# A delta-rule recurrence followed by a token mixer on one core: loads, decay factors, key transposes and mixer products placed differently

## The chip, the cores and the metric

One core of a Trainium2 chip runs the whole program. The metric is device time in microseconds (us). PE is the matmul engine, PEld its weight load, DVE the vector engine, ACT the engine for activation functions, POOL the GpSimd engine; SP only issues DMAs. Each engine works through its own instructions in the order in which they are queued.

## The reference

For 4 batches, 8 heads, 768 tokens and head size 40 (all float32):

```python
for t in range(S):
    y[:, :, t] = einsum('bhd,bhde->bhe', r_t, state)
    Sa = einsum('bhde,bhe->bhd', state, a_t)
    state = state * w_t[:, :, None, :] - einsum('bhd,bhe->bhde', Sa, b_t) + einsum('bhd,bhe->bhde', v_t, k_t)
x = y.transpose(0, 2, 1, 3).reshape(B, S, 320)
theta = x @ w_theta
zr, zi = x * cos(theta), x * sin(theta)
u = x + einsum('ts,bsd->btd', w_tok_r, zr) + einsum('ts,bsd->btd', w_tok_i, zi)
out = u + maximum(u @ w_ch, 0)
```

## The kernel before

The tokens are cut into 24 tiles of 128 (6 to a batch, in order), and one loop, `for i in range(N)`, takes a tile per step with all 8 heads. Inside a tile the recurrence is a masked product of matrices; from tile to tile goes the state `gt`.

- **Load** (`load`, L128): six DMAs of 160 KB for a tile, issued by SP in the order w, k, b, a, r, v. Pool `raw` has three buffers of each, so a tile's buffers come free when the tile three before it has been read. Step i asks for tile i+4.
- **Prepare**: `prep_ln` (ACT, L134) takes the logarithm of w; `prep_csi` sums it with a matmul (L148), takes the Exp (ACT, L151) and multiplies k and b by it (POOL, L155: `kb`); `prep_cse` does the like with the sum that excludes the token itself (L162 to L168, Exp L174) and multiplies a (POOL, L176: `ah`). `prep_rv` (POOL, L143) casts r and v to bf16. `tr_kb`, `tr_rv`, `tr_a` transpose them on PE (L182); the copies out of PSUM are on DVE (L193: `kbT`) and ACT.
- **Scores**: `sc_psiphi` and `sc_lams` (PE, L214) each make two 128x1024 products, and DVE masks them (L222: psi, phi, lamv, lamu). They go in turn through two PSUM tiles named `sc`; everything else in PSUM goes in turn through four named `sm`.
- **Recurrence**: `rec_x0` (L263, L269) gives `nx` (ACT, L273), `rec_nu` gives `nu`, `rec_gt` the next state, `rec_gd` its transpose. `out_y` and `out_xt` make the tile's x and its transpose, one step late.
- **Mixer**: `moe_theta` (PE L410, copy L424) runs for tile i-2 in step i. Twice per batch (at its tile 4, and at tile 1 of the next) `moe_sines` takes cosine and sine of three tiles' theta (ACT, L443), which needs another activation table; `ln_exp_again` (L447) loads the first one again. `moe_z` (POOL, L432: `zr`, `zi`) multiplies them with x one step later, six products in a row. From step 9 on a step has one row block of the mixer, from step 21 on two: `moe_y` (12 matmuls, L453), `moe_ut` (L362) and, a step later, `moe_ch` (L410) and the output DMA.
- **Weights**: after step 0 POOL issues the DMAs of w_theta and w_ch; after each of steps 0 to 5 those of one row block of both token weights (`wtok_load`, L375, two of 128x768). `wtok_trans` (PE L399, DVE L402) transposes a block two steps after its load.
- **Tail**: after the loop the last batch's theta, sines, products and six row blocks are left.

The order in which an engine's instructions are queued is not quite the order of the program: a planner at compile time follows the program but lets a later instruction go first when, by its own estimate of times, the earlier one is not ready. `keep_in_program_order` holds the marked instructions in the program's order. So a cast or product may be queued ahead of one that the program has before it, and then the engine waits for it.

Of the kernel before, what the change touches and what calls it, by code (L numbers as in the profile page):

```python
# [18 lines left out]
def kernel(  # L19
# [63 lines left out]
    for i, t in sorted(to_zero, key=lambda e: e[0]):  # L83
        nc.vector.memset(t, 0.0)

    raw = ctx.enter_context(tc.tile_pool(name="raw", bufs=3))
    exps = ctx.enter_context(tc.tile_pool(name="exps", bufs=4))
    trs = ctx.enter_context(tc.tile_pool(name="trs", bufs=3))
    scs = ctx.enter_context(tc.tile_pool(name="scs", bufs=2))
# [18 lines left out]
    def tile_of(pool, shape, dt, tag):  # L108
        return pool.tile(shape, dt, name=tag, tag=tag)
# [26 lines left out]
    def prep_rv(i):  # L136
        q = tiles[i]
        q.rvb = rv_t[i % NB]
        for j in range(2):
            if i < 2:  # L140
                nc.scalar.copy(out=q.rvb[:, j, :, 0:D], in_=q.rv[:, j])
            else:
                nc.gpsimd.tensor_copy(out=q.rvb[:, j, :, 0:D], in_=q.rv[:, j])  # L143

    def prep_csi(i):
        q = tiles[i]
        csi = tile_of(ps_sm, [128, 512], FP32, "sm")
        nc.tensor.matmul(csi[:, 0:DM], lhsT=ntri_inc, rhs=q.lw[:, :, 0:D],  # L148
                         start=True, stop=True)
        q.invW = tile_of(exps, [128, 1, H, D], FP32, "invW")  # L150
        nc.scalar.activation(out=q.invW.rearrange("p o h d -> p (o h d)"),  # L151
                             in_=csi[:, 0:DM], func=AF.Exp)
        q.kbh = kb_t[i % NB]
        for j in range(2):
            (nc.vector if i < 2 else nc.gpsimd).tensor_tensor(  # L155
                out=q.kbh[:, j, :, 0:D], in0=q.kb[:, j], in1=q.invW[:, 0],
                op=ALU.mult)

    def prep_cse(i):
# [13 lines left out]
        q.Wi = tile_of(exps, [128, DM + 8], FP32, "Wi")
        nc.scalar.activation(out=q.Wi, in_=cse[:, 0:DM + 8], func=AF.Exp)  # L174
        q.ah = ah_t[i % 2]
        (nc.vector if i < 2 else nc.gpsimd).tensor_tensor(  # L176
            out=q.ah[:, :, 0:D], in0=q.a,
            in1=q.Wi[:, 0:DM].rearrange("p (h d) -> p h d", h=H), op=ALU.mult)
# [238 lines left out]
    def moe_theta(i):  # L417

        bi, j = divmod(i, NCH)
        if bi not in ths:  # L420
            ths[bi] = tile_of(mk, [128, NT, DM], FP32, "th")
        tp = tile_of(ps_sm, [128, 512], FP32, "sm")
        mix3(tp[:, 0:DM], tiles[i].xT, wth)
        nc.scalar.copy(out=ths[bi][:, j], in_=tp[:, 0:DM])  # L424

    cs_of = {}

    def moe_z(bi, js):
        cs = cs_of[bi, js[0]]
        for m, j in enumerate(js):  # L430
            for c in range(2):
                nc.gpsimd.tensor_tensor(out=zs[bi][c][:, j], in0=cs[:, c, m],  # L432
                                        in1=tiles[bi * NCH + j].x, op=ALU.mult)

    def moe_sines(bi, js):
        if bi not in zs:
            zs[bi] = (tile_of(mk, [128, NT, DM], BF16, "zr"),
                      tile_of(mk, [128, NT, DM], BF16, "zi"))
        j0, n = js[0], len(js)
        cs = tile_of(mk, [128, 2, 3, DM], FP32, "cs")  # L440
        cs_of[bi, j0] = cs
        for c in range(2):
            tc.keep_in_program_order(nc.scalar.activation(  # L443
                out=cs[:, c, 0:n], in_=ths[bi][:, j0:j0 + n], func=AF.Sin,
                bias=(pi2_col[:, :], 0.0)[c]))
# [61 lines left out]
    prep_cse(1)  # L507
    lv = score(tiles[0].rvT[:, 1], tiles[0].rvT[:, 0])
    tiles[0].lamv = masked("lamv", lv, mask_p)
    tr_kb(1)  # L510
    prep_rv(1)
    tr_rv(1)
    prep_ln(2)
    prev = []
    z_due = None
    for i in range(N):
        bi, ci = divmod(i, NCH)
        yrows = rows_at.get(i, [])
        sines = ci == 4 or (ci == 1 and bi > 0)
        nxt(load, i + 4)  # L520
        rec_x0(i)
        nxt(tr_a, i + 1)
        if i > 1:
            moe_theta(i - 2)
        nxt(prep_csi, i + 2)
        rec_nu(i)
        if i > 0:
            out_y(i - 1)
        nxt(prep_cse, i + 2)
        nxt(sc_psiphi, i + 1)  # L530
        out_nut(i)
        rec_gt(i)
        nxt(ev_phi, i + 1)
        if i > 0:
            out_xt(i - 1)
        due = None
        if sines:
            due = (bi, (0, 1, 2)) if ci == 4 else (bi - 1, (3, 4, 5))
            moe_sines(*due)
            ln_exp_again()  # L540
            busy_act[0] = True
        for m in prev:
            moe_ch(*m)
        nxt(prep_rv, i + 2)
        for m in yrows:
            moe_y(*m)
        nxt(tr_rv, i + 2)
        nxt(tr_kb, i + 2)
        sc_lams(i, i + 1)
        rec_gd(i)  # L550
        for m in yrows:
            moe_ut(*m)
        busy_act[0] = False
        if i == 0:
            moe_weights()
        if i < NCH:
            wtok_load(i)
        if 2 <= i < NCH + 2:
            wtok_trans(i - 2)
        nxt(prep_ln, i + 3)  # L560
        if z_due:
            moe_z(*z_due)
        z_due = due
        prev = yrows
    moe_theta(N - 2)
    moe_sines(B - 1, (3, 4))
    moe_z(B - 1, (3, 4))
    out_y(N - 1)
    for m in prev:
        moe_ch(*m)  # L570
    acc = [tile_of(ps_sc, [128, 2, 512], FP32, "sc") for _ in range(2)]
    yps = [acc[j // 2][:, j % 2, 0:DM] for j in range(4)]
    for j in range(2):
        y_part(yps[j], B - 1, j, range(NT - 1), True, False)
    out_xt(N - 1)
    for j in range(2, 4):
        y_part(yps[j], B - 1, j, range(NT - 1), True, False)
    moe_theta(N - 1)
    moe_sines(B - 1, (5,))
    moe_z(B - 1, (5,))  # L580
    for j in range(NT):
        if j < 4:
            y_part(yps[j], B - 1, j, (NT - 1,), False, True)
            y_evac(yps[j], B - 1, j)
        else:
            moe_y(B - 1, j)
        if j > 0:
            moe_ut(B - 1, j - 1)
        if j > 1:
            moe_ch(B - 1, j - 2)  # L590
    moe_ut(B - 1, NT - 1)
    moe_ch(B - 1, NT - 2)
    moe_ch(B - 1, NT - 1)


# [28 lines left out]
```

## Time and profile before

| | |
|---|---|
| time, median of 3 runs | 260.32 us (259.92 to 261.09) |
| profiled execution: time, span | 262.26 us, 260.5 us |
| busy, of the span | PE 215.0 (83%), DVE 185.4 (71%), ACT 160.4 (62%), POOL 120.9 (46%) |
| loads by SP (queue q1) | 27.54 MB, 59.1% of 16 DMA engines over the span |
| chain that ended last | PE 46%, ACT 15%, issue 12%, DMA 10%, POOL 9% |

The span is what the profiler saw from the first to the last instruction. A step is told here from the end of one `nx` (L273) to the end of the next; step i begins at the end of its own `nx`, and there are 24 of them. A buffer number in a tile's name counts through a ring: `rv_94` to `rv_97` and `kb_90` to `kb_93` are tiles 0 to 3, then 4 to 7, and so on.

### The profile page before, as it was taken

What the parts mean: (1) busy time and instruction counts of PE and PEld (TensorE: products, weight loads), DVE (VectorE), ACT (ScalarE), POOL (GpSimd) and SP (SyncE); (2) the same over time, 40 slices, a digit from 0 to 9 for tenths busy, and PEclk for the clock granted to TensorE, in tenths of its full rate; (3) what the DMA queues carried; (4) which work ended last, traced back from release to release, by engine and by line L of the source; (5) the groups of instructions that cost most, each with busy time, mean ns of one, the idle gap of its engine ahead of it and who ended that gap; (6) DMA issues with size and microseconds to landing.
All of it is one profiled execution on the core that took longest, in us unless ns stands there. A gap on an engine that the chain in (4) does not pass through costs nothing.

```text
span 260.5 us, 8110 instructions
## 1 busy us (share of the span) xinstructions
PE 215.0 (83%) x3368; PEld 167.8 (64%) x3368; DVE 185.4 (71%) x287; ACT 160.4 (62%) x303; POOL 120.9 (46%) x186
## 2 busy tenths in 40 slices
PE   1579968977099969997999899989989999897593
PEld 0457747756067758786777687767777877674361
DVE  5377865887158968897889788978897877750233
ACT  2466645688226867796769576967695838542221
POOL 2009736365735595278427832784177301504200
PEclk9999997999659979999999999999999999999778
DMA  7999999999999898767697579645500001011012
GB/s 128 189 176 149 210 158 195 159 159 169 181 190 168 138 172 154 133 117 136 129 172 138 91 137 169 113 95 110 103 29 4 28 25 35 20 64 40 0 50 101
DMA packets 155685, 30.81 MB, mean 118 GB/s; under 512 B 150401, under 2 KB 155649, under 8 KB 155649
## 3 DMA queue, kind: packets, MB, share of 16 engines
q1 hardware_dynamic: 153216, 27.54, 59.1%
q0 software_dynamic: 2432, 2.77, 6.4%
q8 instruction: 26, 0.43, 0.7%
q14 instruction: 11, 0.08, 0.1%
HBM read 29.13 MB, written 3.93 MB: 127 GB/s over the span
## 4 chain that ended last, share of the span: by engine, by line
PE 46%; ACT 15%; issue 12%; DMA 10%; POOL 9%; DVE 4%; SPq 3%; POOLq 0%; DVEq 0%; ACTq 0%
PE sm L453 10%; DMA raw_rv<-in_r_dram 9%; PE sm L182 7%; PE sc L214 6%; PE sm L410 5%; ACT cs L443 4%; SPq L128 3%; ACT L443 2%; ACT L447 2%; PE sc L453 2%; PE sm L362 2%; PE sm L349 2%; PE sm L278 2%; DVE lamu L222 1%; POOL kb_93 L155 1%
## 5 line engine op out<-in xcount | busy, mean ns | idle before, releaser
L103 ACT COPY rvT<-sm 128x1024 bf16<-128x1024 bf16 x18 | 18.2, 1013 | 26.0 <-PE sm L182 26.0
L453 PE MATMUL sm<-zr,wtok_r 128*128 128x320 bf16 x120 | 33.8, 304 | 0.0
L453 PE MATMUL sm<-zi,wtok_i 128*128 128x320 bf16 x120 | 33.7, 303 | 0.0
L222 DVE TENSOR_TENSOR psi<-sc,mask_p 128x1024 bf16<-128x1024 f32 x24 | 29.3, 1221 | 5.4 <-PE sc L214 5.1
L222 DVE TENSOR_TENSOR phi<-sc,mask_n 128x1024 bf16<-128x1024 f32 x24 | 29.1, 1214 | 0.0
L222 DVE TENSOR_TENSOR lamu<-sc,mask_p 128x1024 bf16<-128x1024 f32 x24 | 29.1, 1214 | 0.0
L222 DVE TENSOR_TENSOR lamv<-sc,mask_p 128x1024 bf16<-128x1024 f32 x24 | 29.1, 1214 | 0.0
L193 DVE COPY kbT<-sm 128x1024 bf16<-128x1024 bf16 x24 | 16.5, 687 | 14.7 <-PE sm L182 14.7
L331 ACT COPY nuT<-sm 128x512 bf16<-128x512 bf16 x24 | 14.0, 585 | 10.9 <-PE sm L182 10.8
L453 PEld LDWEIGHTS <-wtok_r 128*128 128x128 bf16 x144 | 14.4, 100 | 9.6 <-issue 3.9
L453 PEld LDWEIGHTS <-wtok_i 128*128 128x128 bf16 x144 | 14.3, 100 | 7.5 <-issue 1.9
L214 PE MATMUL sc<-aT,kbT 64*128 64x128 bf16 x384 | 18.8, 229 | 0.0
L273 ACT ACTIVATE nx<-sm 128x320 bf16<-128x320 f32 x24 | 10.4, 432 | 11.5 <-PE sm L269 11.5
L103 ACT COPY uT<-sm 128x384 bf16<-128x384 bf16 x18 | 8.5, 483 | 14.1 <-PE sm L362 14.1
L143 POOL CAST rv_96<-raw_rv 128x320 bf16<-128x320 f32 x12 | 5.4, 453 | 24.5 <-DMA raw_rv<-in_r_dram 21.8
L155 POOL TENSOR_TENSOR kb_93<-raw_kb,invW 128x320 bf16<-128x320 f32 x12 | 10.1, 866 | 13.2 <-ACT invW L151 13.2
L424 ACT COPY th<-sm 128x320 f32<-128x320 f32 x24 | 10.6, 441 | 8.6 <-PE sm L410 8.6
L200 ACT COPY aT<-sm 128x512 bf16<-128x512 bf16 x24 | 14.1, 587 | 2.0 <-PE sm L182 2.0
L155 POOL TENSOR_TENSOR kb_91<-raw_kb,invW 128x320 bf16<-128x320 f32 x10 | 8.4, 861 | 14.4 <-ACT invW L151 14.4
L410 PE MATMUL sm<-wch,uT 128*128 128x320 bf16 x72 | 14.3, 313 | 0.2 <-ACT uT L103 0.2
L174 ACT ACTIVATE Wi<-sm 128x328 f32<-128x328 f32 x24 | 10.7, 448 | 5.9 <-PE sm L168 3.1
L214 PEld LDWEIGHTS <-kbT 64*128 64x128 bf16 x384 | 11.9, 99 | 3.7 <-issue 2.9
(332 smaller groups left out, 689.5 us busy)
## 6 DMA issues: line engine op xcount, KB each, us to landing
raw_w<-in_w_dram SPq DMA_DIRECT2D x24, 160.0 KB, 3.8
raw_kb<-in_k_dram SPq DMA_DIRECT2D x24, 160.0 KB, 3.5
raw_kb<-in_b_dram SPq DMA_DIRECT2D x24, 160.0 KB, 3.6
raw_a<-in_a_dram SPq DMA_DIRECT2D x24, 160.0 KB, 3.9
raw_rv<-in_r_dram SPq DMA_DIRECT2D x24, 160.0 KB, 3.8
raw_rv<-in_v_dram SPq DMA_DIRECT2D x24, 160.0 KB, 3.9
out_dram<-oo SPq DMA_DIRECT2D x24, 160.0 KB, 1.8
wtok_row_r<-in_moe_w_tok_r_dram POOLq DMA_DIRECT2D x6, 192.0 KB, 5.1
```

Of the source, the lines that this page charges most:

```text
L103: nc.scalar.copy(out=out, in_=in_)
L155: (nc.vector if i < 2 else nc.gpsimd).tensor_tensor(out=q.kbh[:, j, :, 0:D], in0=q.kb[:, j], in1=q.invW[:, 0], op=ALU.mult)
L174: nc.scalar.activation(out=q.Wi, in_=cse[:, 0:DM + 8], func=AF.Exp)
L182: nc.tensor.transpose(out=dst[:, g * 128:(g + 1) * 128], in_=src[:, 2 * g:2 * g + 2, :].rearrange("p a b -> p (a b)"), identity=ident)
L193: nc.vector.tensor_copy(out=q.kbT.rearrange("p a b -> p (a b)"), in_=pt)
L200: nc.scalar.copy(out=q.aT, in_=pt[:, 0:512])
L214: nc.tensor.matmul(P[:, p, g, :], lhsT=lhs[rows(p), g * 128:(g + 1) * 128], rhs=rhs[rows(p), g * 128:(g + 1) * 128], start=True, stop=True)
L222: nc.vector.tensor_tensor(out=s.rearrange("p a b c -> p (a b) c"), in0=P.rearrange("p a b c -> p (a b) c"), in1=mask.to_broadcast([128, 2 ...
L331: nc.scalar.copy(out=q.nuT, in_=pt[:, 0:512])
L410: nc.tensor.matmul(dst, lhsT=lhs[:, kt, :], rhs=rhs[:, kt, :], start=kt == 0, stop=kt == 2)
L443: tc.keep_in_program_order(nc.scalar.activation(out=cs[:, c, 0:n], in_=ths[bi][:, j0:j0 + n], func=AF.Sin, bias=(pi2_col[:, :], 0.0)[c]))
L453: nc.tensor.matmul(yp, lhsT=wtok[nm][:, sb, j * 128:(j + 1) * 128], rhs=z[:, sb], start=start and n == 0, stop=stop and n == 2 * len(sbs) - 1)
```

## The change

Loads get a fourth buffer, and the row blocks of the token weights are loaded and transposed later (steps 3 to 8 and 6 to 11 instead of 0 to 5 and 2 to 7). `tr_kb` runs for tile i+1 near the head of step i, where it ran for tile i+2 near its end. `prep_csi` stands behind `out_y`, and it reloads the table when sines ran before it. `prep_ln` stands ahead of the sines. `moe_theta` runs for tile i-1 late in the step. The products of three tiles are put behind three steps (two where the batch's rows come next). `th` and `cs` have one buffer. The tail takes the row blocks in another order, and DVE does some of its products.

```diff
-    raw = ctx.enter_context(tc.tile_pool(name="raw", bufs=3))
+    raw = ctx.enter_context(tc.tile_pool(name="raw", bufs=4))
+    mk1 = ctx.enter_context(tc.tile_pool(name="mk1", bufs=1))      # for th and cs
...
     def prep_csi(i):
...
+        if reload[0]:
+            ln_exp_again()
+            reload[0] = False
         q.invW = tile_of(exps, [128, 1, H, D], FP32, "invW")
-        nc.scalar.activation(...)
+        tc.keep_in_program_order(nc.scalar.activation(...))       # Wi in prep_cse too
...
-    def moe_z(bi, js):
-        for m, j in enumerate(js):
-            for c in range(2):
-                nc.gpsimd.tensor_tensor(out=zs[bi][c][:, j], ...)
+    def moe_z(group, m, other=None):
+        for c in range(2):
+            eng = other if other is not None and c == 0 else nc.gpsimd
+            tc.keep_in_program_order(eng.tensor_tensor(out=zs[bi][c][:, js[m]], ...))
...
-    tr_kb(1)                                   # ahead of the loop
     for i in range(N):
...
         nxt(tr_a, i + 1)
-        if i > 1:
-            moe_theta(i - 2)
-        nxt(prep_csi, i + 2)
+        nxt(tr_kb, i + 1)
         rec_nu(i)
         if i > 0:
             out_y(i - 1)
+        nxt(prep_csi, i + 2)
         nxt(prep_cse, i + 2)
...
             out_xt(i - 1)
+        nxt(prep_ln, i + 3)
         if sines:
             moe_sines(*due)
-            ln_exp_again()
+            z_due += [(due, m) for m in range(3)]
+            reload[0] = True
...
         nxt(tr_rv, i + 2)
-        nxt(tr_kb, i + 2)
+        if i > 0:
+            moe_theta(i - 1)
         sc_lams(i, i + 1)
...
-        if i < NCH:
-            wtok_load(i)
-        if 2 <= i < NCH + 2:
-            wtok_trans(i - 2)
-        nxt(prep_ln, i + 3)
-        if z_due:
-            moe_z(*z_due)
+        if 3 <= i < NCH + 3:
+            wtok_load(i - 3)
+        if 6 <= i < NCH + 6:
+            wtok_trans(i - 6)
+        for e in z_due[:1 if ci not in (2, 3) and i < N - 1 else 3]:
+            moe_z(*e)
+            z_due.remove(e)
-    moe_theta(N - 2)
     moe_sines(B - 1, (3, 4))
-    moe_z(B - 1, (3, 4))
+    moe_z((B - 1, (3, 4)), 0)
+    moe_z((B - 1, (3, 4)), 1, nc.vector)
     out_y(N - 1)
...
     for j in range(2):
-        y_part(yps[j], B - 1, j, range(NT - 1), True, False)
+        y_part(yps[j], B - 1, j, range(3), True, False)
     out_xt(N - 1)
+    for j in range(2):
+        y_part(yps[j], B - 1, j, range(3, NT - 1), False, False)
+    moe_theta(N - 1)
+    moe_sines(B - 1, (5,))
+    moe_z((B - 1, (5,)), 0, nc.vector)
     for j in range(2, 4):
         y_part(yps[j], B - 1, j, range(NT - 1), True, False)
-    moe_theta(N - 1)
-    moe_sines(B - 1, (5,))
-    moe_z(B - 1, (5,))
-    for j in range(NT):
-        if j < 4: ...
-        else:
-            moe_y(B - 1, j)
+    for j in range(4, NT):
+        yps.append(tile_of(ps_sm, [128, 512], FP32, "sm")[:, 0:DM])
+        y_part(yps[j], B - 1, j, range(NT - 1), True, False)
+    for j in range(NT + 2):
+        if j < NT: ...                         # the last of six parts, for all rows
```

## Rows read from the trace of the kernel before

**Rows 1.** The page's 40 slices: granted TensorE clock, DMA busy share, in tenths

```profile
PEclk9999997999659979999999999999999999999778
DMA  7999999999999898767697579645500001011012
```

**Rows 2.** Windows between ends of `nx`: length, busy per engine (count), clock, DMA share, GB/s

```profile
19.14:101.16 82.02, 64.73 (x1127) 51.98 (x1126) 60.16 (x77) 51.95 (x100) 50.59 (x79) 0.90 1.02 169
25.74:32.64 6.90, 6.24 (x119) 4.99 (x119) 6.03 (x8) 4.72 (x11) 5.28 (x9) 1.00 1.27 209
...
32.64:44.15 11.51, 8.48 (x133) 6.92 (x132) 7.77 (x11) 5.12 (x12) 5.80 (x10) 0.85 1.00 171
44.15:51.74 7.59, 6.93 (x135) 5.68 (x135) 5.83 (x8) 5.39 (x13) 3.07 (x5) 1.00 0.94 167
...
61.39:76.19 14.80, 8.08 (x122) 6.26 (x121) 6.90 (x9) 4.72 (x11) 10.71 (x17) 0.68 1.09 182
...
126.70:135.18 8.48, 8.28 (x141) 6.54 (x140) 7.28 (x10) 5.38 (x13) 3.35 (x5) 1.00 0.72 138
135.18:143.99 8.81, 7.40 (x134) 6.08 (x133) 8.06 (x11) 8.32 (x14) 6.28 (x9) 1.00 0.75 140
...
223.80:260.50 36.70, 27.12 (x226) 17.61 (x225) 12.21 (x25) 10.42 (x21) 6.00 (x8) 0.87 0.13 46
```

**Rows 3.** DMA queue of the weights: packets, MB, share of 16 engines

```profile
q0 software_dynamic: 2432, 2.77, 6.4%
```

**Rows 4.** Timeline of POOL: start, duration, engine, line, tiles, [idle before, releaser]

```profile
18.81 0.45 POOL L143 CAST rv_96<-raw_rv 128x320 bf16<-128x320 f32 x1 [16.37 <-DMA raw_rv<-in_r_dram]
...
63.63 0.82 POOL L432 TENSOR_TENSOR zr<-cs,x_102 128x320 bf16<-128x320 f32 x1
...
69.47 0.45 POOL L143 CAST rv_94<-raw_rv 128x320 bf16<-128x320 f32 x1 [1.31 <-DMA raw_rv<-in_r_dram]
...
70.52 1.67 POOL L155 TENSOR_TENSOR kb_93<-raw_kb,invW 128x320 bf16<-128x320 f32 x2
...
74.68 0.45 POOL L143 CAST rv_95<-raw_rv 128x320 bf16<-128x320 f32 x1 [1.67 <-DMA raw_rv<-in_r_dram]
```

**Rows 5.** Timeline of PE in step 5

```profile
71.43 0.61 PE L182 MATMUL sm<-ident,kb_93 128*128 128x128 bf16 x4 [6.33 <-POOL kb_93 L155]
```

**Rows 6.** Timeline of ACT at the end of step 13, one with sines

```profile
141.90 1.28 ACT L447 ACT_TABLE_LOAD   x1
143.19 0.47 ACT L134 ACTIVATE lw_86<-raw_w 128x320 bf16<-128x320 f32 x1
143.57 0.42 ACT L273 ACTIVATE nx<-sm 128x320 bf16<-128x320 f32 x1
```

**Rows 7.** Timeline of PE at the same place

```profile
144.04 0.57 PE L410 MATMUL sm<-wth,xT_3059 128*128 128x320 bf16 x3 [1.43 <-ACT nx L273]
```

**Rows 8.** Groups by line, weight transposes and `kbT`: busy us, mean ns | idle before

```profile
L399 PE MATMUL sm<-ident,wtok_row_r 128*128 128x128 bf16 x36 | 4.0, 249 | 0.0
L402 DVE COPY wtok_r<-sm 128x768 bf16<-128x768 bf16 x6 | 3.3, 546 | 0.0
L193 DVE COPY kbT<-sm 128x1024 bf16<-128x1024 bf16 x24 | 16.5, 687 | 14.7 <-PE sm L182 14.7
```

**Rows 9.** Timeline at the head of step 12, DVE and PE

```profile
126.44 1.21 DVE L222 TENSOR_TENSOR lamu<-sc,mask_p 128x1024 bf16<-128x1024 f32 x1
128.47 0.49 DVE L353 TENSOR_TENSOR x_113<-sm,Wi 128x320 bf16<-128x320 f32 x1 [0.82 <-PE sm L349]
128.53 0.51 PE L214 MATMUL sc<-aT,kbT 64*128 64x128 bf16 x12
```

**Rows 10.** Chain that ended last, in the tail: start, duration, engine, tile, line

```profile
232.87 1.28 ACT L443
...
242.02 0.43 ACT th L424
...
252.61 1.63 PE sm L453 x12
```

More of the change, by code (lines that the diff above doesn't have):

```diff
@@ L143, in prep_rv @@
                 nc.gpsimd.tensor_copy(out=q.rvb[:, j, :, 0:D], in_=q.rv[:, j])
+    reload = [False]
     def prep_csi(i):
@@ L149, in prep_csi @@
                          start=True, stop=True)
+        if reload[0]:
+            ln_exp_again()
+            reload[0] = False
         q.invW = tile_of(exps, [128, 1, H, D], FP32, "invW")
-        nc.scalar.activation(out=q.invW.rearrange("p o h d -> p (o h d)"),
-                             in_=csi[:, 0:DM], func=AF.Exp)
+        tc.keep_in_program_order(nc.scalar.activation(
+            out=q.invW.rearrange("p o h d -> p (o h d)"), in_=csi[:, 0:DM],
+            func=AF.Exp))
         q.kbh = kb_t[i % NB]
@@ L173, in prep_cse @@
         q.Wi = tile_of(exps, [128, DM + 8], FP32, "Wi")
-        nc.scalar.activation(out=q.Wi, in_=cse[:, 0:DM + 8], func=AF.Exp)
+        tc.keep_in_program_order(nc.scalar.activation(
+            out=q.Wi, in_=cse[:, 0:DM + 8], func=AF.Exp))
         q.ah = ah_t[i % 2]
@@ L420, in moe_theta @@
         if bi not in ths:
-            ths[bi] = tile_of(mk, [128, NT, DM], FP32, "th")
+            ths[bi] = tile_of(mk1, [128, NT, DM], FP32, "th")
         tp = tile_of(ps_sm, [128, 512], FP32, "sm")
@@ L426 @@
     cs_of = {}
-    def moe_z(bi, js):
+    def moe_z(group, m, other=None):
+        bi, js = group
         cs = cs_of[bi, js[0]]
-        for m, j in enumerate(js):
-            for c in range(2):
-                nc.gpsimd.tensor_tensor(out=zs[bi][c][:, j], in0=cs[:, c, m],
-                                        in1=tiles[bi * NCH + j].x, op=ALU.mult)
+        for c in range(2):
+            eng = other if other is not None and c == 0 else nc.gpsimd
+            tc.keep_in_program_order(eng.tensor_tensor(
+                out=zs[bi][c][:, js[m]], in0=cs[:, c, m],
+                in1=tiles[bi * NCH + js[m]].x, op=ALU.mult))
     def moe_sines(bi, js):
@@ L439, in moe_sines @@
         j0, n = js[0], len(js)
-        cs = tile_of(mk, [128, 2, 3, DM], FP32, "cs")
+        cs = tile_of(mk1, [128, 2, 3, DM], FP32, "cs")
         cs_of[bi, j0] = cs
@@ L514 @@
     prev = []
-    z_due = None
+    z_due = []
     for i in range(N):
@@ L535 @@
             out_xt(i - 1)
-        due = None
+        nxt(prep_ln, i + 3)
         if sines:
@@ L555 @@
             moe_weights()
-        if i < NCH:
-            wtok_load(i)
-        if 2 <= i < NCH + 2:
-            wtok_trans(i - 2)
-        nxt(prep_ln, i + 3)
-        if z_due:
-            moe_z(*z_due)
-        z_due = due
+        if 3 <= i < NCH + 3:
[5 more added lines that the diff above has]
+            z_due.remove(e)
         prev = yrows
-    moe_theta(N - 2)
     moe_sines(B - 1, (3, 4))
-    moe_z(B - 1, (3, 4))
+    moe_z((B - 1, (3, 4)), 0)
+    moe_z((B - 1, (3, 4)), 1, nc.vector)
     out_y(N - 1)
@@ L573 @@
     for j in range(2):
-        y_part(yps[j], B - 1, j, range(NT - 1), True, False)
+        y_part(yps[j], B - 1, j, range(3), True, False)
     out_xt(N - 1)
+    for j in range(2):
[3 more added lines that the diff above has]
+    moe_z((B - 1, (5,)), 0, nc.vector)
     for j in range(2, 4):
         y_part(yps[j], B - 1, j, range(NT - 1), True, False)
-    moe_theta(N - 1)
-    moe_sines(B - 1, (5,))
-    moe_z(B - 1, (5,))
-    for j in range(NT):
-        if j < 4:
+    for j in range(4, NT):
+        yps.append(tile_of(ps_sm, [128, 512], FP32, "sm")[:, 0:DM])
+        y_part(yps[j], B - 1, j, range(NT - 1), True, False)
+    for j in range(NT + 2):
+        if j < NT:
             y_part(yps[j], B - 1, j, (NT - 1,), False, True)
             y_evac(yps[j], B - 1, j)
-        else:
-            moe_y(B - 1, j)
-        if j > 0:
+        if 0 < j <= NT:
             moe_ut(B - 1, j - 1)
@@ L590 @@
             moe_ch(B - 1, j - 2)
-    moe_ut(B - 1, NT - 1)
-    moe_ch(B - 1, NT - 2)
-    moe_ch(B - 1, NT - 1)
 _INS = ['r', 'k', 'v', 'w', 'a', 'b', 'moe_w_theta', 'moe_w_tok_r', 'moe_w_tok_i', 'moe_w_ch']
```

## The prediction, made before the change was run

> **What bounds the kernel now.** I read four views in turn. The page's slices [rows 1] show DMA at 9 tenths until about 90 us and a granted clock that drops three times in that stretch. The windows between the ends of `nx` [rows 2] then split the span: from 19.14 to 101.16 nine steps take 82.0 us at a DMA share of 1.02, with PE busy for only 64.7 of them; from step 9 on PE is the bound (8.28 busy of 8.48 in step 12; step 13 takes 8.81); the tail behind the last `nx` is 36.7 us, of which PE is idle for 9.6. So there are three stages with three limits: loads, PE, and a chain of small things.
>
> The timelines say why the early steps are uneven. Step 1 takes 6.90, step 3 takes 7.59, but step 2 takes 11.51 and step 5 takes 14.80 [rows 2]. In step 5 PE waits 6.33 us for `kb_93` [rows 5], the keys of tile 7. Those were not late themselves: on POOL the products stand behind six mixer products that begin at 63.63 and behind the cast of `rv_94`, which is tile 8, and that cast waits for its load until 69.47 [rows 4]. So the key product of the nearer tile waits for the load of the farther one, and PE, in order, waits for both. The clock of that step is 0.68 [rows 2], a mixture of its two levels (1.2 and 2.4 GHz), and it falls behind the idle time, so the wait also makes the next matmuls slower.
>
> **The change, part by part. Loads.** POOL's cast of r shows when a tile lands where the cast waits for it: tile 2 at 18.81, tile 9 at 74.68 [rows 4]. That is 55.9 us for 7 tiles and, between them, all the weights, which took 6.4% of 16 engines' span [rows 3], or 16.7 us. A tile alone is thus (55.9 - 16.7) / 7 = 5.6 us, less than any early step. The bytes do not change; what changes is that the token weights (six blocks of about 2.4 us each) come after step 3, so that tiles 4 to 7 are no longer pushed back by them, and that a fourth buffer lets SP ask a step sooner. Step 8 casts tile 10: 18.8 + 8 x 5.6 + 16.7 = 80.3 us if every weight is ahead of it. Step 5 of the old trace needed 6.7 us from the landing of tile 8's r (69.47) to the end of `nx` (76.19), so step 9 can begin at 87.0. By computing alone, six steps at 6.9 and three at 7.6 (those that transpose weights) give 19.1 + 64.2 = 83.3. I take the later, 87, against 101.16: **-14**. The ends: -18 if computing is the limit, and -3 if casts are still queued two tiles ahead of the key products (two more tiles, +11.2).
>
> **Key transposes and products.** With `tr_kb` a step later, the key product has about a whole step until PE wants it, so a POOL queue that is late by a few us no longer stops PE; this is what makes -14 possible and is not counted twice. The two products at a time (1.6 us instead of 4.8, from 0.8 each [rows 4]) hide beside PE as before. What is late next is the cast of r and v, whose transposes stay in the same step. `prep_ln` moves ahead of the sines, and behind it on ACT stand the step's remaining copies; it needs the w of tile i+3, which is first of the six loads and lands some five loads, 4.7 us, before its tile is complete, so I cost it at nothing; without that cover it is the one-tile delay inside the range above.
>
> **Weights transposed later.** Steps 9 to 11 get these on top of their row blocks, and PE is the bound there. The group shows 4.0 us for six blocks of one matrix [rows 8], so 1.3 us per step for both, part of it at the lower clock; with DVE's two copies of 0.55 beside it. I take 1.0 per step: **+3** (0 if they fill idle PE, 4 at the row's price). The steps 2 to 5 that lose them are limited by loads, so nothing comes back.
>
> **Sines.** In step 13 ACT loads the table at 141.90 for 1.28 us, takes the logarithm for 0.47, and only then `nx` at 143.57 [rows 6]; PE waits 1.43 for it [rows 7]. Both go from ahead of `nx`. The logarithm comes back ahead of the sines, so about 1.0 remains. The reload now stands ahead of the late Exp, where it holds two of the four `sm` tiles longer while queued behind it on ACT are Exp, Exp and the copy of `nuT`; none of these is wanted before the end of the step. I cost it at 0.3, between 0 and the 1.28 of the row. Net -0.7 for steps 10, 13, 16 and 19: **-2.8** (-5.7 to +5). For steps 4 and 7 the loads decide.
>
> The trace has the reload at 1.28 us with the next ACT instruction at its end [rows 6]. The Trainium skill, "ScalarE: Activation LUTs", section "What ACT_TABLE_LOAD costs", speaks against a switch in a tight place: about 1.28 us and a drain of 1.38 us on top. By it the moved reload would hold the Exp for 2.7, and the sum would lose up to 4 x 1.4 more; the row has no such gap, and I go by the row.
>
> **Tail.** Nothing is prepared after the sines of step 22, so the table is not loaded back, and the 1.28 us at 232.87 on the chain [rows 10] goes. The copy of theta at 242.02 ran between two batches of sines with no load ahead of it [rows 10], so plain copies live with that table. Of the four products that POOL has there DVE takes one, at POOL's 0.8 [rows 4]: -0.8. Row blocks 4 and 5, 12 matmuls or 1.63 each [rows 10], stood behind the last products; now 20 of those 24 (20 x 1.63 / 12) run while PE waits for them: -2.7. Together with theta of tile 22 inside the loop **-5** (from -9.6, all of PE's idle time [rows 2], to +1 if two held `sm` tiles stall the last copies).
>
> The trace has no DVE product beside a POOL one. The Trainium skill, "SBUF — State Buffer", section "Who interferes with whom", says that a DVE instruction with both inputs in SBUF contends with a GpSimd instruction that reads SBUF. By it the split products would run one after the other and the sum would be about 0.5 worse twice, most of it under the 40 matmuls that now stand there.
>
> **Sum.** -14 + 3 - 2.8 - 5 = -18.8. The profiled execution took 262.26 (span 260.5 and 1.8 around it), which gives 243.5; the median of the runs is 0.74% lower, so 241.7. All good ends together are -33 (227), all bad ones +7 (267).
>
> **Rivals.** First, the inversion stays: the planner still queues casts of r and v of farther tiles ahead of nearer key products. For it: it did so in every early step [rows 4], it guesses when loads land, and a fourth buffer lets it guess earlier still. Against it: keys have a step more. Then -5 instead of -14 early: 250.6.
>
> Second, more table loads: `nx` and `nu` now run between sines and reload, and no row shows an ACT product there, only the copy of theta [rows 10]. A load for each of seven groups is 7 x 1.28 = 9.0, which also gives 250.6.
>
> Third, slower: the copy of `kbT` on DVE (0.69 [rows 8]) now stands at the head of the step, behind `lamu`, and the first scores of the step need it. In step 12 `lamu` ends at 127.65 [rows 9]; a copy right behind it ends at 128.34, and the 12 later scores begin at 128.53 [rows 9], so 0.2 is to spare. If instead the copy is queued behind x (0.49, begun at 128.47 [rows 9]), it ends at 129.65 and PE waits 1.1 in each of 23 steps, 26 us: a net +7, or 267. It decides from 18.8 / 23 = 0.8 us per step.
>
> Fourth, the change does not do what it says: the loads stay pinned as they were since the same bytes have to come by about 90 us, the early gain is nought, and the transposes of +3, an unhidden reload and the tail cancel: 260.
>
> **Chances.** Forecast 0.62 (alone 235 to 248), inversion 0.20, table loads 0.05, slower by `kbT` 0.08, no change 0.05. Faster by over 0.5%, which is about what a measurement of this kernel can tell from no change: 0.62 + 0.20 + 0.05 = 0.87; within 0.5% 0.05; slower 0.08. The range of 8 in 10, 231 to 255, takes in the first three and leaves out the last two and a little below.
>
> **What would show it.** Right: step 9 begins between 83 and 92 us; no PE wait for `kb` over 1 us after step 1; the clock stays at its upper level from 20 us on; the steps of sines have less than 0.6 of idle PE; steps 9 to 11 are about 1 us longer than the same steps later; the tail behind the last `nx` takes 30 to 33 us and has no table load. Wrong: POOL waiting for a load of r with a key product queued behind it for more than a step, DVE or PE idle at the head of each step until `kbT`, more ACT table loads than 14 in all, or a tail of 36 us.

## The result and the profile after

The changed kernel takes 246.78 us (median of 4 runs, 245.36 to 247.79) against 260.12 before (4 runs, 259.16 to 261.09): a ratio of 0.9483 [0.9424, 0.9543]. The forecast was 241.7, with a range of 231 to 255. The profiled execution took 246.64, its span 244.9 against 260.5, so 15.6 of the span went, where the sum had 18.8. Of two kernels below, rv_first and sines_old, the profiled execution was a slow one (1.7 to 1.8% above the fastest of the same kernel), so of these two only steps at full clock are compared.

The page of the kernel after: slices of PE's busy share, granted clock and DMA share, and the queue of the weights, to be laid beside [rows 1, 3].

```profile
PE   1476899974299699989999999989999999989992
PEclk9999999999569979999999999999999999999997
DMA  7999998999999999999979987654100000111012
q0 software_dynamic: 2432, 2.77, 7.4%
```

The weights' packets took 18.1 us of 16 engines (7.4% of 244.9; 16.7 before), and the transfers stay dense further into the span. Of the holes in PE's row one deep one is left, in the tenth and eleventh slices (55 to 67 us), and the clock falls in the eleventh.

The windows between ends of `nx`, columns as in [rows 2]. In order: steps 0 to 8; step 6; steps 9 to 11; step 10; steps 12 to 22; step 13; the tail.

```profile
15.42:92.47 77.05, 60.14 (x1095) 47.64 (x1095) 60.01 (x73) 53.08 (x103) 46.80 (x73) 0.91 1.07 176
59.25:75.49 16.24, 9.38 (x138) 7.58 (x139) 7.43 (x9) 5.26 (x13) 8.24 (x14) 0.68 1.11 183
92.47:119.72 27.25, 25.29 (x439) 20.62 (x439) 24.24 (x35) 19.14 (x36) 18.58 (x28) 1.00 1.00 169
101.02:111.49 10.47, 9.29 (x158) 7.50 (x158) 10.06 (x17) 7.13 (x13) 5.74 (x9) 1.00 0.97 165
119.72:214.28 94.56, 91.19 (x1539) 72.69 (x1538) 82.62 (x113) 69.41 (x131) 47.94 (x67) 1.00 0.46 90
128.17:136.14 7.97, 7.50 (x129) 5.95 (x129) 7.76 (x11) 7.16 (x12) 4.97 (x8) 1.00 0.98 179
214.28:244.88 30.60, 23.95 (x223) 15.84 (x222) 13.10 (x27) 8.82 (x18) 4.56 (x6) 0.96 0.15 55
```

The first `nx` ends at 15.42 (19.14 before), step 9 begins at 92.47 (101.16 before [rows 2]), the tail is 30.60 (36.70). One step stands out as step 5 did before: step 6 takes 16.24 at a clock of 0.68. The next two fences are POOL and PE in that step, columns as in [rows 4].

```profile
56.97 0.81 POOL L441 TENSOR_TENSOR zr<-cs,x_102 128x320 bf16<-128x320 f32 x1
...
59.23 0.78 POOL L441 TENSOR_TENSOR zi<-cs,x_103 128x320 bf16<-128x320 f32 x1
62.65 0.45 POOL L144 CAST rv_94<-raw_rv 128x320 bf16<-128x320 f32 x1 [2.64 <-DMA raw_rv<-in_r_dram]
63.06 1.67 POOL L162 TENSOR_TENSOR kb_93<-raw_kb,invW 128x320 bf16<-128x320 f32 x2
64.69 0.86 POOL L184 TENSOR_TENSOR ah_89<-raw_a,Wi 128x320 bf16<-128x320 f32 x1
```

```profile
65.60 0.61 PE L190 MATMUL sm<-ident,ah_89 128*128 128x128 bf16 x4 [6.89 <-POOL ah_89 L184]
66.01 1.06 PE L190 MATMUL sm<-ident,kb_93 128*128 128x128 bf16 x8
```

This is the queue of [rows 4] and the wait of [rows 5] again, one step later: four mixer products, then the cast of tile 8 that waits 2.64 for its load, and only then the key and `a` products of tile 7, whose Exp had been done since 56.33 (next fence). PE needs `ah_89` and `kb_93` in this very step and waits 6.89 us.

ACT in steps 5 and 13, to [rows 6]:

```profile
54.26 1.28 ACT L457 ACT_TABLE_LOAD   x1
55.55 0.44 ACT L157 ACTIVATE invW<-sm 128x320 f32<-128x320 f32 x1
55.89 0.44 ACT L181 ACTIVATE Wi<-sm 128x328 f32<-128x328 f32 x1
...
132.06 1.28 ACT L453 ACT_TABLE_LOAD   x1
133.35 1.10 ACT L453 ACTIVATE cs<-th,pi_col 128x960 f32<-128x960 f32 x1
134.35 0.99 ACT L453 ACTIVATE cs<-th 128x960 f32<-128x960 f32 x1
135.37 0.42 ACT L432 COPY th<-sm 128x320 f32<-128x320 f32 x1
135.69 0.44 ACT L281 ACTIVATE nx<-sm 128x320 bf16<-128x320 f32 x1
```

`nx` now follows the sines with one copy between. The groups of ACT's table loads, 14 in all (16 before):

```profile
L453 ACT ACT_TABLE_LOAD x7 | 9.0, 1283 | 0.1
L457 ACT ACT_TABLE_LOAD x6 | 7.7, 1283 | 0.1
L492 ACT ACT_TABLE_LOAD x1 | 1.3, 1283 | 0.7 <-PEq L617 0.7
```

PE's waits over the whole span (total, times, longest) show what is late now; `kb_90` (4.8) and `lw_86` (4.1), not shown, lie ahead of step 0.

```profile
PE sm L190 <- POOL ah_89 L184: 6.9, 1, 6.9
...
PE sm L190 <- ACT th L432: 2.8, 4, 1.7
PE sm L190 <- POOL rv_96 L144: 2.0, 1, 2.0
PE sm L271 <- ACT th L432: 1.9, 1, 1.9
...
PE sm L357 <- DVE lamu L230: 0.6, 3, 0.2
```

The two waits of 1.7 and 1.9 for `th` are steps 4 and 7: theta's copy stands behind table load and sines on ACT.

### The profile page after: what moved, and what is told of

Read it like the earlier page. It is cut to its first block, busy times and chain, and to the rows that moved or that the text cites. A ratio compares the mean times of both kernels' runs of the same rounds, so it can differ in the third digit from the quotient of the medians.

```text
span 244.9 us, 8109 instructions
## 1 busy us (share of the span) xinstructions
PE 206.4 (84%) x3368; PEld 161.5 (66%) x3368; DVE 188.4 (77%) x289; ACT 157.7 (64%) x301; POOL 119.7 (49%) x184
## 4 chain that ended last, share of the span: by engine, by line
PE 52%; ACT 12%; DMA 10%; DVE 7%; POOL 7%; issue 6%; SPq 5%; POOLq 0%; ACTq 0%; DVEq 0%
PE sm L463 11%; PE sm L190 9%; PE sc L222 7%; PE sm L418 6%; SPq L129 5%; DMA raw_rv<-in_v_dram 5%; DVE lamu L230 3%; ACT cs L453 3%; DMA raw_rv<-in_r_dram 2%; DVE lamv L230 2%; PE sm L370 2%; PE sc L463 2%; PE sm L357 2%; ACT L453 2%; DMA raw_kb<-in_k_dram 2%
## 5 line engine op out<-in xcount | busy, mean ns | idle before, releaser
L463 PE MATMUL sm<-zi,wtok_i 128*128 128x320 bf16 x120 | 33.1, 299 | 0.0
L463 PE MATMUL sm<-zr,wtok_r 128*128 128x320 bf16 x120 | 33.1, 299 | 0.0
L104 ACT COPY rvT<-sm 128x1024 bf16<-128x1024 bf16 x18 | 18.2, 1011 | 19.1 <-PE sm L190 19.0
L162 POOL TENSOR_TENSOR kb_92<-raw_kb,invW 128x320 bf16<-128x320 f32 x12 | 10.1, 865 | 26.0 <-ACT invW L157 26.0
L222 PE MATMUL sc<-aT,kbT 64*128 64x128 bf16 x384 | 16.1, 229 | 0.0
L357 PEld LDWEIGHTS <-lamu 128*128 128x128 bf16 x192 | 13.4, 98 | 3.2 <-DVE lamu L230 3.1
L162 POOL TENSOR_TENSOR kb_93<-raw_kb,invW 128x320 bf16<-128x320 f32 x12 | 10.1, 860 | 10.3 <-ACT invW L157 10.3
L432 ACT COPY th<-sm 128x320 f32<-128x320 f32 x24 | 10.3, 429 | 6.5 <-PE sm L418 6.4
L354 PEld LDWEIGHTS <-lamv 128*128 128x128 bf16 x192 | 14.0, 97 | 0.6 <-issue 0.5
L418 PE MATMUL sm<-wch,uT 128*128 128x320 bf16 x72 | 13.4, 299 | 1.2 <-ACT invW L157 0.6
L347 PE MATMUL sm<-gd,rvT 128*128 128x80 bf16 x80 | 13.1, 200 | 0.4 <-DVE gd L102 0.4
```

The costliest lines, as they stand in the source:

```text
L104: nc.scalar.copy(out=out, in_=in_)
L162: (nc.vector if i < 2 else nc.gpsimd).tensor_tensor(out=q.kbh[:, j, :, 0:D], in0=q.kb[:, j], in1=q.invW[:, 0], op=ALU.mult)
L222: nc.tensor.matmul(P[:, p, g, :], lhsT=lhs[rows(p), g * 128:(g + 1) * 128], rhs=rhs[rows(p), g * 128:(g + 1) * 128], start=True, stop=True)
L354: nc.tensor.matmul(o, lhsT=q.lamv[:, p, g, :], rhs=q.kbh[:, 0, h, 0:D], start=first, stop=False, skip_group_check=True)
L357: nc.tensor.matmul(o, lhsT=q.lamu[:, p, g, :], rhs=q.kbh[:, 1, h, 0:D], start=False, stop=True, skip_group_check=True)
L418: nc.tensor.matmul(dst, lhsT=lhs[:, kt, :], rhs=rhs[:, kt, :], start=kt == 0, stop=kt == 2)
```

## The experiments

Twelve kernels, each with 4 runs, compared with the kernel before on the same chip. "Early" is from the first `nx` to the beginning of step 9. Stages are of one profiled execution each.

| | median us | ratio | first `nx` | early | 9 to 11 | 12 to 22 | tail |
|---|---|---|---|---|---|---|---|
| before | 260.12 | 1 | 19.1 | 82.0 | 25.5 | 97.1 | 36.7 |
| after | 246.78 | 0.9483 [0.9424, 0.9543] | 15.4 | 77.1 | 27.3 | 94.6 | 30.6 |
| pool_order | 253.83 | 0.9742 [0.9664, 0.9820] | 15.4 | 77.9 | 29.9 | 97.5 | 30.6 |
| rv_first | 241.27 | 0.9220 [0.9127, 0.9312] | 16.0 | 72.6 | 27.3 | 94.6 | 30.6 |
| kb_old | 251.29 | 0.9634 [0.9566, 0.9702] | 18.8 | 76.5 | 28.1 | 94.5 | 30.6 |
| weights_early | 249.26 | 0.9559 [0.9488, 0.9631] | 15.9 | 81.1 | 24.4 | 94.4 | 30.6 |
| few_loads | 240.62 | 0.9221 [0.9155, 0.9286] | 15.5 | 69.4 | 28.1 | 94.6 | 30.6 |
| tail_old | 251.28 | 0.9655 [0.9604, 0.9706] | 16.0 | 76.0 | 27.2 | 95.2 | 33.6 |
| sines_old | 253.92 | 0.9724 [0.9664, 0.9784] | 15.5 | 77.8 | 29.9 | 99.7 | 31.7 |
| rvf_few | 238.51 | 0.9160 [0.9116, 0.9204] | 15.6 | 68.2 | 27.2 | 94.6 | 30.6 |
| rvf_ln | 239.64 | 0.9223 [0.9180, 0.9266] | 16.1 | 68.7 | 27.3 | 95.2 | 30.6 |
| rvf_ln_tr | 241.77 | 0.9287 [0.9232, 0.9343] | 15.3 | 70.9 | 26.8 | 95.1 | 32.2 |
| raw3 | 246.51 | 0.9484 [0.9435, 0.9534] | 15.4 | 77.3 | 27.5 | 94.6 | 30.6 |
| z_burst | 248.10 | 0.9522 [0.9466, 0.9577] | 15.9 | 75.6 | 27.3 | 94.8 | 30.6 |

How far one execution can be trusted shows in tail_old, whose edit lies all behind the loop: its first `nx` ends at 15.99, its early stage takes 75.99 and its step 6 takes 14.05, where the change has 15.42, 77.05 and 16.24. Differences of 1 us in the early stage, or of 2 us in step 6, are not read as effects.

**The order of POOL's queue.** pool_order holds the casts of r and v and the products `kb` and `ah` on POOL in the program's order:

```diff
-                nc.gpsimd.tensor_copy(out=q.rvb[:, j, :, 0:D], in_=q.rv[:, j])
+                tc.keep_in_program_order(
+                    nc.gpsimd.tensor_copy(out=q.rvb[:, j, :, 0:D], in_=q.rv[:, j]))
...
+            if i >= 2:
+                tc.keep_in_program_order(ins)          # kb; the same for ah
```

> The changed kernel with POOL's casts of r and v and its products kb and ah also held in program order, nothing left out. Theory A (order): step 6 of the changed kernel (16.24 us, PE waiting 6.89 for ah of tile 7) is long because POOL's cast of r of tile 8 is queued ahead of kb and ah of tile 7, so that a near tile waits for a far load. Then step 6 falls to about 9 us, the end of nx of step 9 comes at 85 to 88 instead of 92.5, and the time is 239 to 243, less some loss in later steps, where the cast now always stands behind kb and ah of its own tile. Theory B (supply): tile 8 was simply not there, and whatever is queued first, its transposes stop PE in the same step. Then nx of step 9 stays at 91 to 94 and the time at 245 to 249.

Neither theory had this: it is slower than the change itself, though step 6 falls to 8.78. The long wait is gone, and many short ones stand in its place. The first of PE's waits, and POOL in step 6:

```profile
PE sm L195 <- POOL rv L145: 16.7, 14, 2.3
```

```profile
66.60 1.69 POOL L163 TENSOR_TENSOR kb<-raw_kb,invW 128x320 bf16<-128x320 f32 x2 [2.14 <-ACT invW L158]
68.24 0.87 POOL L187 TENSOR_TENSOR ah<-raw_a,Wi 128x320 bf16<-128x320 f32 x1
69.05 0.85 POOL L145 CAST rv<-raw_rv 128x320 bf16<-128x320 f32 x2
```

The casts now wait behind products that wait for an Exp, and PE wants the cast tile in the same step. So the program's own order is as wrong as the planner's, the other way round. rv_first keeps the pins and moves the cast to the head of the step, so that it is queued ahead of products of the same tile and behind those of the tile before:

```diff
         nxt(load, i + 4)
+        nxt(prep_rv, i + 2)
         rec_x0(i)
...
             moe_ch(*m)
-        nxt(prep_rv, i + 2)
```

> As the one before, but the cast of r and v of tile i+2 stands at the head of step i, ahead of that tile's kb and ah; nothing left out. Theory A: no POOL instruction waits for a tile farther than the one that the step prepares, so step 6 falls to about 9 us as well, and since the cast is early the later steps lose nothing: 238 to 242. Theory B: 245 to 249, as the changed kernel.

0.9220 against 0.9483: the order of this one queue is worth 6.8 us (0.0263 x 260), and the time is 241.27, as Theory A had it. In its trace PE waits at most 2.5 for a cast. A new wait is 3.6 for `th` in step 4, because the logarithm ahead of the sines waits for its load (ACT):

```profile
49.07 0.47 ACT L135 ACTIVATE lw<-raw_w 128x320 bf16<-128x320 f32 x1 [2.08 <-DMA raw_w<-in_w_dram]
```

**Is it the products or the load?** few_loads leaves the changed kernel's queue alone and takes transfers away:

```diff
-        if 3 <= i < NCH + 3:
-            wtok_load(i - 3)
+        if i == 3:
+            wtok_load(0)                     # block 0 stands for all six
+            for tb in range(1, NT):
+                for nm in ("r", "i"):
+                    wrows[nm, tb] = wrows[nm, 0]
```

> The changed kernel with one row block of the token weights loaded (at step 3) and used for all six, so 5 of 6 of these loads are left out and the output is not the reference's. Theory A (order): the far load that POOL stands behind in step 6 lands some 5 us sooner, so step 6 falls from 16.2 to 9 to 11 us though the queue is the same, and the time is 239 to 242. Theory B' (the mixer products and the late Exp ahead of kb make the 6.9 us, not the load): step 6 stays over 14 us and the time over 244.

POOL there, and the window of step 6:

```profile
53.91 1.54 POOL L441 TENSOR_TENSOR zr<-cs,x 128x320 bf16<-128x320 f32 x2
55.41 1.54 POOL L441 TENSOR_TENSOR zi<-cs,x 128x320 bf16<-128x320 f32 x2
57.86 0.45 POOL L144 CAST rv<-raw_rv 128x320 bf16<-128x320 f32 x1 [0.90 <-DMA raw_rv<-in_r_dram]
58.27 1.68 POOL L162 TENSOR_TENSOR kb<-raw_kb,invW 128x320 bf16<-128x320 f32 x2
```

```profile
61.64:68.89 7.25, 6.66 (x129) 5.20 (x127) 6.96 (x9) 5.02 (x13) 4.33 (x7) 1.00 1.04 178
```

Same queue, same four products ahead of the cast, but the load comes sooner: step 6 takes 7.25 at full clock instead of 16.24, and the time is 240.62. In the change the products end at 60.01 (59.23 + 0.78), 2.64 before the cast can start, so there they delay nothing that the load does not delay as well. few_loads alone does not single out the far tile, since the nearer loads come sooner in it too (the products begin at 53.91 and not at 56.97); rv_first, with all loads left in, does that. z_burst has all six products one step later, as they were before the change. The six end at 61.23, the cast still waits 0.98 for its load, and step 6 takes 13.81:

```diff
-            z_due += [(due, m) for m in range(3)]
+            z_new = [(due, m) for m in range(3)]
...
-        for e in z_due[:1 if ci not in (2, 3) and i < N - 1 else 3]:
+        for e in z_due:
             moe_z(*e)
-            z_due.remove(e)
+        z_due = z_new
+        z_new = []
```

> The changed kernel with the mixer products in a row of six, one step after the sines, as before. If the spread matters, key products stand behind 4.8 us of them instead of 1.6 to 3.2, most of all in steps 5 and 8, and the time is 248 to 252. If with a step of slack for the keys it does not matter, 245.5 to 247.5, and less if the queue in step 5 happens to put the key product ahead of the far cast.

Its median lies at the lower end of the first range, but its ratio lies within the interval of the change's. The time does not decide here; the queue does.

**How much is left in the loads.** rvf_few is both, rv_first and the one block of few_loads.

> The kernel with POOL's casts at the head of the step and everything on POOL in program order, with one row block of the token weights loaded and used for all six (5 of 6 of these loads left out, the output is not the reference's). If supply is what is left once the order is mended, nx of step 9 comes at 78 to 82 instead of 88.6 and the time is 231 to 235. If the steps are then limited by computing, 86 to 89 and 238 to 241.

It falls between the two accounts. Its ratio is 0.006 below that of rv_first, with overlapping intervals, and step 9 begins at 83.78, 0.9 before the 84.70 of rvf_ln below, which has all its loads. Two of its steps:

```profile
38.84:45.18 6.34, 6.17 (x126) 4.92 (x124) 6.10 (x8) 5.12 (x12) 4.89 (x8) 1.00 1.05 174
45.18:53.38 8.20, 6.17 (x124) 4.79 (x122) 7.87 (x10) 7.04 (x14) 4.32 (x6) 1.00 1.05 180
```

Step 3 is 6.34, with 0.17 of it idle on PE; step 4, with sines and as much PE work, is 8.20. So from step 2 on the loads no longer set these steps; in steps 4 and 7 ACT's sines do (PE waits 1.9 for `th` in each). Steps 0 and 1 still wait for casts and products. rvf_ln puts the logarithm behind the sines again, through step 8, where loads can be late, and rvf_ln_tr transposes the weights a step earlier as well.

```diff
-        nxt(prep_ln, i + 3)
+        if i > 8:
+            nxt(prep_ln, i + 3)
...
+        if i <= 8:
+            nxt(prep_ln, i + 3)
```

> The kernel with POOL's casts at the head of the step and everything on POOL in program order, and prep_ln at the end of the step up to step 8 (ahead of the sines from step 9 on); nothing left out. In that kernel ACT waited 2.1 us in step 4 and 2.4 in step 6 for the w of a tile three ahead, with nx queued behind. If those waits cost time of their own, steps 4 and 6 lose 2 to 4 us each of their 10.4 and 11.3, and the time is 236 to 239. If supply alone is the limit there, other waits take their place: 240 to 242.

The time is 239.64, and the ratio, 0.9223, is that of rv_first (0.9220), so a gain over rv_first is not shown. Step 6 in it, with as many matmuls as in the change:

```profile
59.53:67.25 7.72, 7.05 (x138) 5.62 (x137) 6.95 (x9) 5.37 (x12) 6.57 (x11) 1.00 1.06 178
```

And the second edit, of rvf_ln_tr:

```diff
-        if 6 <= i < NCH + 6:
-            wtok_trans(i - 6)
+        if 5 <= i < NCH + 4:
+            wtok_trans(i - 5)
+        if i == NCH + 3:
+            wtok_trans(NCH - 1)
```

> As the one before, with the weight transposes one step sooner (steps 5 to 9, the last two both in step 9), so that steps 10 and 11 have none; nothing left out. Step 10 is one with sines and was 10.5 us where steps 13, 16 and 19 are 8.0, DVE being busy for all but 0.4 of it. If each block costs what the early-weights kernel showed (2.9 us for three), steps 9 to 11 lose 1 to 1.5 us net and the time is 235 to 238; a wait of PE for a block that has not landed yet would take that back.

No gain is shown (0.9287 against 0.9223, overlapping): step 10 falls from 10.46 to 8.23, but step 9, with two blocks, rises from 8.56 to 10.21, and the tail takes 32.2 at a granted clock of 0.91 in this execution, where rvf_ln has 30.6 at 0.98.

**The change's parts, each undone alone.** The place of `moe_theta`, the place of `prep_csi` and the single buffers of `th` and `cs` were not undone alone. kb_old:

```diff
+    tr_kb(1)                                   # ahead of the loop
...
-        nxt(tr_kb, i + 1)
...
+        nxt(tr_kb, i + 2)                      # behind tr_rv
```

> The changed kernel with tr_kb put back: for tile i+2 late in step i. My account says that the key transposes' step of slack is what lets POOL be late without stopping PE: with the late Exp the key product ends some 5 us into the step, so PE would wait for kb in nearly every step, 0.5 to 1.5 us, and more in the early ones: 255 to 270. The rival (slack is worth nothing, loads and sines made the gain): 245 to 249.

0.015 more, 3.9 us, which lies between the two accounts. Its PE waits, and the window of steps 12 to 22:

```profile
PE sm L190 <- POOL kb L162: 10.3, 6, 6.8
```

```profile
123.40:217.88 94.48, 89.51 (x1530) 71.95 (x1530) 81.87 (x112) 69.67 (x131) 47.93 (x67) 1.00 0.45 87
```

The later `tr_kb` gives 3.4 us ahead of step 0 (first `nx` at 18.83 without it). From there to step 9 it gives nothing that shows, 77.1 against 76.5: the waits for keys go (10.3 in six places) and the one for `ah_89` comes. In the steady steps it neither costs nor gives: 94.56 against 94.48.

weights_early loads the blocks at steps 0 to 5 and transposes them at 2 to 7:

```diff
-        if 3 <= i < NCH + 3:
-            wtok_load(i - 3)
-        if 6 <= i < NCH + 6:
-            wtok_trans(i - 6)
+        if i < NCH:
+            wtok_load(i)
+        if 2 <= i < NCH + 2:
+            wtok_trans(i - 2)
```

> The changed kernel with the token weights back at steps 0 to 5 (loads) and 2 to 7 (transposes). By my account of the loads tiles 4 to 7 come later again, by up to 9 us for tile 7, so that nx of step 9 ends at 94 to 100, and steps 9 to 11 give back about 1 us each without the weight transposes: in sum 246 to 253. The rival (the same bytes have to come by then, their order does not matter): nx of step 9 stays at 92.5 and the 2 to 3 us of transposes come off: 243 to 245.

The stages to step 9 and from 9 to 11, and between them steps 2 to 5 of this kernel and of the change:

```profile
15.90:97.05 81.15, 64.16 (x1138) 51.65 (x1139) 62.40 (x79) 53.41 (x104) 50.64 (x78) 0.89 1.09 179
33.70:64.69 30.99, 26.35 (x515) 21.27 (x512) 28.17 (x36) 23.58 (x46) 18.68 (x29) 1.00 1.11 185
32.12:59.25 27.13, 23.64 (x467) 18.52 (x464) 24.68 (x30) 23.13 (x45) 16.68 (x27) 1.00 1.04 174
97.05:121.43 24.38, 23.24 (x407) 18.61 (x405) 21.62 (x29) 19.01 (x37) 14.93 (x22) 1.00 1.00 173
```

Step 9 begins 4.6 later (97.05 against 92.47), 4.1 of it behind the first `nx`. Little of that is the order of the loads: steps 2 to 5, which have transposes in this kernel and none in the change, take 3.9 longer at full clock, and 2.7 of that is PE's busy time, while step 6 with its long wait takes 16.07 against 16.24. So most of the early gain of the later weights comes from the transposes that left these steps; what the later loads alone are worth is not shown. Behind step 9 the transposes cost 2.9 (24.38 to 27.25), nearly all of it in step 10 (8.06 to 10.47), the one with sines. In the ratios 2 us are left, with overlapping intervals. raw3 is `bufs=3` in place of `bufs=4`.

> The changed kernel with three buffers for the loads. By the profile of the changed kernel the DMA share is 9 tenths or more to 130 us, so if the fourth buffer is what keeps SP ahead, nx of step 9 comes 2 to 6 us later and the time is 249 to 253. If the loads are limited by the DMA engines and not by free buffers, 246 to 248.

The same ratio to 0.0001: the fourth buffer moved nothing that these runs can tell.

tail_old has the old order of the tail, all products on POOL; theta of tile 22 stays in the loop:

```diff
-    moe_z((B - 1, (3, 4)), 0)
-    moe_z((B - 1, (3, 4)), 1, nc.vector)
+    for m in range(2):
+        moe_z((B - 1, (3, 4)), m)
...
-        y_part(yps[j], B - 1, j, range(3), True, False)
+        y_part(yps[j], B - 1, j, range(NT - 1), True, False)
     out_xt(N - 1)
...                                             # row blocks 4 and 5 last, as before
-    moe_z((B - 1, (5,)), 0, nc.vector)
+    moe_z((B - 1, (5,)), 0)
```

> The changed kernel with the tail in the old order: all four products on POOL, row blocks 4 and 5 wholly behind the last products; the table is still not loaded back after step 22 and theta of tile 22 stays in the loop. If the new order of the row blocks and the split products made the tail's gain (6.1 us from 36.7 to 30.6), the tail is 34 to 36 us and the time 250 to 252. If the table load and the earlier theta made it, the tail is 31 to 32 and the time 247 to 248.

```profile
214.41:247.99 33.58, 24.15 (x223) 16.02 (x222) 12.15 (x25) 8.82 (x19) 5.74 (x8) 0.99 0.14 50
```

The tail lies between the two accounts. The time, 251.28, lies in the range of the first, but the ratios differ by 4.5 us, and only 3.0 of that is the tail in this execution; the rest is not placed. Of the tail's 6.1, order and split products are 3.0 (33.58 to 30.60). What stayed in tail_old, theta of tile 22 in the loop and no table load in the tail, comes with 3.1 (36.70 [rows 2] to 33.58), but so does the clock: it was 0.87 before and 0.99 here, and PE was busy for 27.12 with 226 matmuls before and for 24.15 with 223 here. These two are not separated. sines_old undoes the late reload and the early logarithm:

```diff
-        nxt(prep_ln, i + 3)                   # ahead of the sines
...
+            ln_exp_again()
-            reload[0] = True
...
+        nxt(prep_ln, i + 3)                   # end of the step
```

> The changed kernel with the table loaded back right behind the sines and prep_ln at the end of the step, as before; nothing left out. My account: steps 13, 16 and 19 go from 8.0 back to 8.8 us and the tail gets a table load of 1.3, 4 us in all; against that ACT no longer waits for a load ahead of the sines of steps 4 and 7, worth up to 2: 248 to 251. The rival (the sines' part is hidden): 245 to 247.

Its window of step 13, at full clock:

```profile
131.89:140.97 9.08, 7.44 (x129) 5.94 (x129) 8.54 (x13) 8.41 (x14) 6.59 (x10) 1.00 0.99 189
```

9.08 against 7.97: 1.1 to 1.2 for each of steps 13, 16 and 19 (9.1, 9.2, 9.1 against 8.0, 8.1, 8.0). It has 16 table loads, two more, one of them in the tail, which is 1.1 longer. That is 4.5 of the 6.3 that the ratios differ by (0.0241 x 260). The rest stays open: steps 11, 17 and 20, each right behind one with sines, ran at a clock of 0.82 to 0.83 in this execution and can't be compared.

## Why the prediction was right, and what was mis-sized

The sum was -18.8; the spans gave -15.6. The time fell in the range partly by luck: the stage that the largest term was about gained 5.0, which is what the first rival gave the early part, and 3.7 ahead of step 0, which no term had, with 1.1 more in the tail, made up for part of what was missing. By its terms:

- **Loads, -14: the mis-sized term.** Step 9 begins 8.7 earlier, not 14. The step that failed is "a POOL queue that is late by a few us no longer stops PE": with keys a step later PE waited for `ah_89` instead, and kb_old, without that edit, is no slower from step 0 to 9. Of the 8.7, 3.7 come ahead of step 0 (kb_old shows that the key transpose does that), and the steps from there take 5.0 less, 77.05 for 82.02 [rows 2]. By weights_early 4.1 of these 5.0 come with the later weights, and there mostly from the transposes that left steps 2 to 5; "nothing comes back" from those was the second thing that failed. The forecast began step 9 at 87.0; 92.47 is 5.5 later. Step 6 alone explains more than that: 16.24 where rvf_ln, with as many matmuls, takes 7.72, so 8.5, of which 6.2 is more idle time and 2.3 more busy time at the lower clock (9.38 for 7.05); in the execution of tail_old it would be 6.3. The first rival, that casts of farther tiles still go ahead of nearer products, was right in step 6; it had been priced at 9 over all nine steps. On POOL the mixer products and the weight DMAs are held in program order in the change, but not the casts and key products, and that is what rv_first mends. By few_loads the trigger is the load's landing; by pool_order a pin alone is no cure.
- **The supply rate.** 87.0 by bandwidth was no bound: rvf_ln begins step 9 at 84.70, near the 83.3 of "computing alone". That floor was near 83.78, where rvf_few begins step 9, by errors that cancel: the start is 3.5 earlier, and the steps take 68.2 and not 64.2. Steps 0, 1, 4 and 7 take 8.2, 8.6, 8.2 and 9.1; "For steps 4 and 7 the loads decide" was wrong, since PE waits for `th` there.
- **The fourth buffer** was named as part of the gain; with raw3 no gain from it shows.
- **Weights transposed later, +3:** 2.9 by weights_early, so the size is right. But it is not 1.0 in each of three steps by PE's time, as I had argued: 2.4 of it are in step 10, where DVE is busy 10.06 of 10.47 with the copies behind the masks, and 0.9 of PE's 1.2 idle there is a wait for `gd`, a copy that DVE makes in steps with sines.
- **Sines, -2.8:** steps 12 to 22 gave 2.5, step 13 went from 8.81 [rows 2] to 7.97; undone, it costs 1.1 to 1.2 per step, more than the 0.7 predicted. In step 10 it shows only in weights_early (8.06 for 8.92 before), where no transposes stand in that step. The wait for `nx` of [rows 7] (1.43) has become one of 0.4 for `th`. The reload took 1.28 with the Exp at its end (54.26, 55.55). The Trainium skill, "ScalarE: Activation LUTs", section "What ACT_TABLE_LOAD costs", would have had 1.38 more for a drain. The load agrees; no row here shows that drain.
- **Tail, -5:** -6.1, in the range given. Order and split, priced at 3.5, gave 3.0. Load and theta, priced at 1.5, came with 3.1, in which the tail's higher clock has a share that is not known.
- **Rivals two and three** did not come: 14 table loads, none for `nx` between sines and reload; the wait for `lamu` or a copy at the head of a steady step is 0.2 at most, where 0.8 per step would have decided.
- **The signs.** The tail of 30 to 33 us and the 14 table loads came. Step 9 began at 92.47 and not by 92, the clock did not stay up (0.68 in step 6), and step 10 had 1.2 of idle PE and not under 0.6.

The split products in the tail: DVE's first and POOL's first after the change, then POOL's first in tail_old, where DVE has none.

```profile
223.70 0.49 DVE L441 TENSOR_TENSOR zr<-cs,x_112 128x320 bf16<-128x320 f32 x1
```

```profile
223.75 1.10 POOL L441 TENSOR_TENSOR zr<-cs,x_111 128x320 bf16<-128x320 f32 x1 [8.30 <-ACT cs L453]
```

```profile
223.88 0.79 POOL L441 TENSOR_TENSOR zr<-cs,x 128x320 bf16<-128x320 f32 x1 [8.30 <-ACT cs L453]
```

Beside DVE's product POOL's took 1.10, alone 0.79. The Trainium skill, "SBUF — State Buffer", section "Who interferes with whom", says that such a pair contends. In this one pair it does, by 0.31: from the start of the first to the end of the second are 1.15 us, where one after the other would be 1.28 (0.49 + 0.79).

## What to carry to other kernels

When an engine's queue is ordered from estimates, look for the instruction that waits for a far transfer and ask what stands behind it. Moving the consumer one step later did not help here from step 0 to 9; the wait moved with it. Pins cured the inversion only together with a place in the program that was right for both sides: the pins alone cost 6.7 us, the pins and one moved line gained 6.8. Where waits are uneven, look for the worst step before working with bytes over rate: one wait of 6.9 and its slow clock made up more than the whole miss. And when work leaves a stage, count what it took there: steps 2 to 5 gave back 3.9 that had been put at nothing.

## What the runs showed that was not expected

- The clock costs a good part of a wait again. In step 6 of the change 138 matmul instructions took 9.38 us behind 6.89 of waiting (granted 0.68, a mixture of 1.2 and 2.4 GHz); in rvf_ln the same number took 7.05 at 1.00.
- The wait for a copy of theta behind the sines is 0.4 in steady steps and 1.7 and 1.9 in early ones. The early ones have no row block of the mixer beside it; that this is the reason was not tested.
- The DMA share of the early stage is 1.02 before [rows 2], 1.07 after and 1.03 in rvf_ln (68.65 us by its window), while the stage fell from 82.0 to 77.1 and 68.7: a share near 1 did not mean that transfers were the bound.
